# Second product of a leaky-ReLU MLP after linear attention: o of the preceding block in steps between h's, one outer Strassen product at a time over all chunks, four of seven by two levels

## The chip, the cores and the metric

One core of a Trainium2 chip. The time is the device time of one execution in microseconds (us). Its engines are named as in the profile: PE (TensorE matmul), PEld (its weight load), DVE (VectorE), ACT (ScalarE), POOL (GpSimd), SP (SyncE, which here only issues DMAs). MB are millions of bytes, KB are 1024 bytes.

## The reference, cut to what matters

```python
kv = np.einsum('bhsd,bhse->bhde', k, v)          # b=8, h=8, s=576, d=64, float32
out = np.einsum('bhsd,bhde->bhse', q, kv)
out = out / np.sqrt(np.mean(out * out, axis=-1, keepdims=True) + 1e-06) * g_norm
x = out.transpose(0, 2, 1, 3).reshape(4608, 512)
h = x @ w_in                                      # 512 x 2048
g = np.maximum(0.01 * h, h)
return g @ w_out                                  # 2048 x 512; out is 4608 x 512 float32
```

## The kernel before, in words

**Blocks and chunks.** The 4608 tokens are nine blocks of 512. For each block the kernel computes h = x w_in, g = leaky ReLU of h, and o = g w_out. The 2048 columns of h are taken in four chunks (NC) of 512: two groups of 128 from the first half of w_in's columns and two from the second. A chunk is a 2 x 2 matrix of quadrants, and so are its rows of w_out, so both products can be done by Strassen's method with seven products instead of eight. Names 11, 12, 21, 22 are quadrants; products have the numbers 1 to 7, and sums of quadrants are their operands. Block 0 is done directly, without Strassen, while the attention of the first tokens starts. Block 1 uses one level for h and for o.

**h by two levels.** From block 2 on, h of a chunk is done by two levels (`product_h_two`, line 930): seven steps, one for each inner product k, and in each step seven matmuls of 128 x 128 x 128, one for each outer product. The sums of w_in that they need are made once during block 1 (`combine`, line 702) and kept in DRAM. They come back as pieces of 448 KB, one for each step, into a ring of five places (`read`, line 737, with the DMA on line 741): when a step's matmuls are done, its place is free and SP issues the load of the piece five steps later. Results go into four PSUM banks, ha and hb or hc and hd; copies to SBUF are ACT's, adds are DVE's. Then DVE adds the outer products up to the quadrants of g, ACT applies the leaky ReLU, and POOL makes four sums of g (`sums_of`, line 839).

**o by one level, mostly.** o of a chunk (`product_o`, line 973) runs two steps of lag behind, one o step after each h step: seven products of four matmuls with 256 columns (128 x 128 weights). After every product, DVE adds the bank to the block's output quadrant in SBUF; the first chunk's are ACT's copies. The four sums of w_out's quadrants are made by POOL in block 1 and written to DRAM; from block 2 on they are read back, two DMAs of 512 KB a chunk (`sides_w2`, line 662, DMA on line 673). For 26 of the chunks, product 2 is done by two levels by the class `Second` (line 905): one more matmul of 128 columns in each h step, with its own small sums on POOL (`inner_g`, `inner_w2`) and a DVE add of 128 columns.

**Attention between.** The next block's x is made in the meantime: loads of q, k and v (lines 130 and 159; q in four DMAs for each pair of heads), DVE's transposes of q (line 455), matmuls for kv and for q kv, the norm on ACT and DVE. Steps of this work are put into fixed slots (`FINE_SLOTS`, line 1113). A slot is one h step; a block has 28. DVE and POOL then make the outer and inner sums of x (`sides_x`, line 752).

**What sets the order.** `pin` (line 90) keeps an engine's instructions in program order, so in the steady part each engine runs the order that the main loop (lines 1136 to 1222) writes down. SP issues nearly all DMAs, in one order: pieces for h, sums of w_out, loads for the attention. An issue that waits holds up those behind it.

```python
def read(to):
    nonlocal n_read
    while n_read < min(to, len(reads)):
        c, k = reads[n_read]
        pin(nc.sync.dma_start(w_place(n_read), w1_dram[c][:, SLOT[k], :, :]))
        n_read += 1
```

Of the kernel before, what the change touches and what calls it, by code (L numbers as in the profile page):

```python
# [23 lines left out]
def kernel(  # L24
# [39 lines left out]
    P = 128  # L64
# [19 lines left out]
    xpool = ctx.enter_context(tc.tile_pool(name="xpool", bufs=3))  # L84
    gpool = ctx.enter_context(tc.tile_pool(name="gpool", bufs=2))
    opool = ctx.enter_context(tc.tile_pool(name="opool", bufs=2))
# [4 lines left out]
    steady = first_done = in_line = False  # L91
# [6 lines left out]

    NW = U * NE * P
    w1_all = consts.tile([P, 2 * NC * NW], F32, name="w1_all")  # L100
    stage = consts.tile([P, 3 * NW], F32, name="stage")
    pairs = consts.tile([P, 4 * NW], F32, name="pairs")
    g_all = [consts.tile([P, 4 * U * N2], F32, name=f"g_{i}") for i in range(2)]

    def view(t, lo, *shape):
        n = 1
        for d in shape:
            n *= d
        t = t[:, lo:lo + n]
        names = "abcd"[:len(shape)]  # L110
        return t.rearrange(f"p ({' '.join(names)}) -> p {' '.join(names)}",
                           **dict(zip(names, shape))) if len(shape) > 1 else t
# [49 lines left out]
    def load_first():  # L162

        early = xpool.tile([P, NE * NT], F32, tag="xT", name="early")
# [25 lines left out]
    def make_ident():  # L190
# [9 lines left out]
    w2_sb = [[consts.tile([P, U, DM], F32, name=f"w2_{h}_{c}") for c in range(NC)]  # L200
             for h in range(2)]

    spare_homes = itertools.cycle(("gs1", "gs2", "gs3", "gs4"))

    def spare(n, name, dtype=F32):

        return gpool.tile([P, n], dtype, tag=next(spare_homes), name=name)
# [97 lines left out]
    def block(i):  # L305
        if i not in xTs:
            xTs[i] = xpool.tile([P, NE, NT], F32, tag="xT", name="xT")
        return xTs[i]
# [48 lines left out]
    def outputs(b, lo, hi, e, sums, kv=None):  # L357
# [8 lines left out]
        for l in range(2):  # L366
            sq = t2k(n, "sq" if e else f"sum{l}")
            nc.scalar.activation(sq, o_ps[l], func=AF.Square)
            if e == 0:
                sums.append(sq)  # L370
            else:
                in_turn(nc.vector.tensor_add(sums[l], sums[l], sq))
        for l in range(2):
            nc.scalar.activation(x[:, 2 * l + e, :], o_ps[l], func=AF.Copy, scale=g_sb[:, e:e + 1])

    def divide(lo, hi, sums):
# [3 lines left out]
        for l in range(2):  # L380
# [4 lines left out]
            if l:  # L385
                act = nc.scalar.activation(rms, rms, func=AF.Sqrt, scale=1.0 / D, bias=eps_sb)
                if first_done:
                    pin(act)
# [3 lines left out]
        for l in range(2):  # L392
            t = t2k(n, "spread")
            nc.scalar.copy(t.rearrange("p (a i) -> p a i", i=E),
                           rms[:, l, :].unsqueeze(2).to_broadcast([P, n // E, E]))
# [9 lines left out]
    def both_outputs(b, lo, hi, sums, kv=None):  # L405
# [8 lines left out]
        for l in range(2):  # L414
            sq = t2k(2 * n, "sq").rearrange("p (e n) -> p e n", e=2)
            nc.scalar.activation(sq, o_ps[l], func=AF.Square)
            sums.append(t2k(n, f"sum{l}"))
            in_turn(nc.vector.tensor_add(sums[l], sq[:, 0, :], sq[:, 1, :]))
        for l in range(2):
            for e in range(2):  # L420
                nc.scalar.activation(x[:, 2 * l + e, :], o_ps[l][:, e, :], func=AF.Copy,
                                     scale=g_sb[:, e:e + 1])
# [24 lines left out]
    def attention(b, apart=True, fine=False):  # L447
# [48 lines left out]
        for tail in (0, 0, 0, 0, 0, 1, 0, 0, 1, 1, 1, 1, 1, 1):  # L496
            next(tails[tail])
            yield
# [141 lines left out]
    def sides_w1(c):  # L640
# [9 lines left out]
        def more():  # L650
# [6 lines left out]
    w2_dram = [[dram.tile([P, 2, U, N2], F32, name=f"w2_{c}_{i}") for i in range(2)]  # L657
               for c in range(NC)]
    t12, t34 = pair(2, 2, U, N2), pair(3, 2, U, N2)
    writes = []  # L660

    def sides_w2(n):


# [5 lines left out]
        def sums(i):  # L670
            t = (t12, t34)[i]
            if n >= NC:
                pin(nc.sync.dma_start(t, w2_dram[c][i]))
                return
# [6 lines left out]
            if (n, i) == (NC - 1, 1):  # L681

                writes.append((w2_dram[c][i], t))
            else:
                pin(nc.sync.dma_start(w2_dram[c][i], t))
        return {1: b11, 2: b21, 3: b22, 5: t12[:, 0], 6: t12[:, 1], 7: t34[:, 0],
                4: t34[:, 1]}, sums


# [3 lines left out]
    INTO = {1: (0, 0), 2: (0, 0), 6: (0, 1), 3: (0, 1), 7: (1, 1), 5: (1, 1), 4: (1, 0)}  # L693
# [36 lines left out]
    reads = [(c, k) for _ in range(2, NB) for c in range(NC) for k in ORDER]  # L730
    RING = 5
    n_read = 0

    def w_place(n):
        return view(w1_all, n % RING * NG, 7, P)

    def read(to):
        nonlocal n_read
        while n_read < min(to, len(reads)):
            c, k = reads[n_read]  # L740
            pin(nc.sync.dma_start(w_place(n_read), w1_dram[c][:, SLOT[k], :, :]))
            n_read += 1

    qa = view(w1_all, RING * NG, 4, 4, P)
    qc = pair(0, 4, 3, P)
    xt1 = [work.tile([P, 2, N2], F32, tag="xt1", name="xt1"),
           view(w1_all, RING * NG + 24 * P, 2, N2)]
    xt24 = [work.tile([P, 2, 2, N2], F32, tag="xt24", name="xt24"),
            view(w1_all, RING * NG + 16 * P, 2, 2, N2)]
    xi = view(stage, 0, 3, 7, P)  # L750

    def sides_x(i):


        x = xTs.pop(i)
        b11, b12 = x[:, :2, :N2], x[:, :2, N2:]
        b21, b22 = x[:, 2:, :N2], x[:, 2:, N2:]
        home = i % 2 if i > 1 else 0
        t1, t2, t4 = xt1[home], xt24[home][:, 0], xt24[home][:, 1]
        if i == 1:  # L760
            t4 = opool.tile([P, 2, N2], F32, tag="o", name="xt4", bufs=6)
# [11 lines left out]
        for js, y in (((1, 7), upper), ((2, 3), lower),  # L773
                      ((6, 4), xt24[home].rearrange("p t r (v n) -> p t r v n", v=2)),
# [9 lines left out]
        def inner(kind):  # L784
            for y11, y12, y21, y22, t1, t2, t4 in batches:
                if kind == 0:
                    add(nc.gpsimd, t1, y12, y11, True)
                    add(nc.gpsimd, t2, y22, t1, True)
                elif kind == 1:
                    add(nc.gpsimd, y12, y22, y12, True)  # L790
                else:
                    add(nc.gpsimd, t4, y21, t2, True)
# [3 lines left out]
    def strassen(tags, left, right, done, order=ORDER, pieces=None):  # L796

        banks = {}  # L800
        for i in order:

            if i is None:
                yield
                continue
# [4 lines left out]
            if pieces and b == tags[0]:  # L810
                if i == 1:
                    homes = [bank] + [ps_m.tile([P, 2, N2], F32, tag=t, name=f"o_{t}")
                                      for t in ("ha", "hc")]
                    ends = [t.rearrange("p u n -> p (u n)")[:, :cols.stop - cols.start]
                            for t, (_, cols) in zip(homes, pieces)]
                for to, (part, cols) in zip(ends, pieces):
                    for r in range(2):
                        matmul(to, lhsT=left(i, part, r), rhs=right(i, part, r)[:, cols],
                               start=(i == 1 and r == 0), stop=(r == 1), skip_group_check=True)
                done(i, ends)  # L820
                yield
                continue
# [8 lines left out]
    def relu(t, src=None):  # L831
        nc.scalar.activation(t, t if src is None else src, func=AF.Prelu, alpha=SLOPE)  # L832
# [6 lines left out]
    def sums_of(c, to):  # L839

        g11, g21, g22, g12 = g_of(c)
        s1, s2, s3, s4 = (gpool.tile([P, 4, P], F32, tag=f"gs{i}", name=f"gs{i}")
                          for i in range(1, 5))
# [37 lines left out]
    gi = view(pairs, 12 * P, 4, P)  # L881

    def inner_w2(c):
        y = w2_sb[1][c]
        t1, t2, t3, t4 = (w2_sb[0][c][:, u, N2 + s * P:N2 + s * P + P]
                          for u in range(2) for s in range(2))
        y11, y12, y21, y22 = (y[:, u, s * P:s * P + P] for u in range(2) for s in range(2))
        add(nc.gpsimd, t1, y12, y11, True)
        add(nc.gpsimd, t2, y22, t1, True)
        add(nc.gpsimd, t3, y22, y12, True)  # L890
        add(nc.gpsimd, t4, y21, t2, True)

    def inner_g(c, half):

        g = g_of(c)[3]
        a11, a21, a12, a22 = (g[:, n, :] for n in range(4))
        s1, s2, s3, s4 = (gi[:, n, :] for n in range(4))
        if half == 0:
            add(nc.gpsimd, s1, a21, a22)
            add(nc.gpsimd, s2, s1, a11, True)  # L900
        else:
            add(nc.gpsimd, s3, a11, a21, True)
            add(nc.gpsimd, s4, a12, s2, True)

    class Second:


        def __init__(self, n, o, finish):
            self.n, self.o, self.finish = n, o, finish
            c = n % NC  # L910
            g, y = g_of(c)[3], w2_sb[1][c]
            ts = [w2_sb[0][c][:, u, N2 + s * P:N2 + s * P + P]
                  for u in range(2) for s in range(2)]
            self.left = {1: g[:, 0, :], 2: g[:, 2, :], 4: g[:, 3, :],
                         **{k: gi[:, at, :] for at, k in enumerate((5, 6, 7, 3))}}
            self.right = {1: y[:, 0, :P], 2: y[:, 1, :P], 3: y[:, 1, P:N2],
                          **{k: ts[at] for at, k in enumerate((5, 6, 7, 4))}}

        def product(self, k, bank):
            matmul(bank, lhsT=self.left[k], rhs=self.right[k], start=False, stop=True,  # L920
                   skip_group_check=True)

        def done(self, k, bank):
# [331 lines left out]
```

## Time and profile before

| | us |
|---|---|
| median of three runs | 917.37 (916.73 to 917.72) |
| span of the profiled execution, first to last instruction | 915.5 |
| PE busy | 909.1 |
| DVE, ACT, POOL busy | 628.2, 327.6, 367.0 |
| DMA moved in the span | 200.06 MB, mean 219 GB/s |

The profiled execution's own time is its span of 915.5 us and what lies around it, launch and end, which no instruction shows; the median of the runs is 1.9 us above the span. A row of a group of instructions reads: line, engine, operation, out<-in by the program's names, shapes, how many; then busy time and the mean of one in ns; then the engine's idle time before them and who ended it. A row of the timeline reads: start, length, engine, line, operation, operands, how many are merged. In rows of waits the first engine waited for the second: total us, times, longest. In rows of DMA issues the last number is the median time in us from issue to landing. The program's matmul in 32-bit floats appears as two MATMUL records.

### The profile page before, as it was taken

To read this page: it belongs to the slowest core of one execution; us is meant where nothing else is said; L and a number is where in the kernel's file an instruction comes from. 1 tells how busy PE (TensorE), PEld (TensorE's weight loads), DVE (VectorE), ACT (ScalarE), POOL (GpSimd) and SP (SyncE) were. 2 spreads that over 40 slices of the span, in tenths; PEclk is the share of its full clock that TensorE was granted. 3 is DMA by queue.
4 is the path that set the end of the run, shared out by engine and by line. 5 is a ranking of instruction groups with operands and counts; after the bars stand their busy time and mean duration, and the time that the engine had idled before them with its cause. 6 is when DMAs were issued, how large, how long until landed. Compare 5 with 4: busy or idle time off the path is not lost.

```text
span 915.5 us, 18030 instructions
## 1 busy us (share of the span) xinstructions
PE 909.1 (99%) x6976; PEld 775.6 (85%) x6976; DVE 628.2 (69%) x1168; ACT 327.6 (36%) x645; POOL 367.0 (40%) x440
## 2 busy tenths in 40 slices
PE   8999999999999999999999999999999999999998
PEld 5444448888998999899999999999999999999997
DVE  5876985587457876587756786678659755755565
ACT  5454533242135233533343324332343333223330
POOL 2000246977633472226321642264226422642222
DMA  9999908895599678877896689658765676667632
GB/s 267 243 243 237 239 35 258 263 304 167 175 360 286 224 213 263 235 233 211 255 261 216 219 250 263 230 179 227 224 184 176 188 221 200 184 187 223 199 107 92
DMA packets 90229, 200.06 MB, mean 219 GB/s; under 512 B 9888, under 2 KB 42272, under 8 KB 90144
## 3 DMA queue, kind: packets, MB, share of 16 engines
q1 hardware_dynamic: 79680, 187.04, 69.5%
q10 hardware_dynamic: 10016, 10.69, 3.4%
q8 instruction: 56, 0.92, 0.4%
q0 software_dynamic: 448, 1.18, 0.3%
q14 instruction: 29, 0.24, 0.1%
HBM read 172.39 MB, written 26.48 MB: 217 GB/s over the span
## 4 chain that ended last, share of the span: by engine, by line
PE 95%; DMA 2%; DVE 1%; POOL 1%; issue 0%; ACT 0%; ACTq 0%; DVEq 0%; POOLq 0%
PE o_a L118 18%; PE o_c L118 18%; PE h_ha L118 11%; PE h_hb L118 11%; PE h_hc L118 8%; PE h_hd L118 8%; PE o_acc L118 6%; PE h_ps L118 6%; PE o_ps L118 3%; PE h_a L118 1%; PE h_c L118 1%; PE kv_ps L118 1%; DMA pairs<-in_v_dram 1%; PE h_b L118 1%; PE h_d L118 1%; DMA w<-pairs 1%
## 5 line engine op out<-in xcount | busy, mean ns | idle before, releaser
L636 POOL TENSOR_TENSOR gs<-g 128x512 f32<-128x512 f32 x64 | 81.7, 1277 | 253.3 <-ACT g L832 253.3
L832 ACT ACTIVATE g<-g 128x512 f32<-128x512 f32 x124 | 78.2, 631 | 130.4 <-DVE g L636 130.4
L951 ACT COPY w_all<-h_ha 128x512 f32<-128x512 f32 x84 | 48.9, 582 | 173.9 <-PE h_ha L118 160.5
L118 PE MATMUL o_a<-pairs,gs 128*128 128x256 f32 x384 | 91.3, 381 | 0.0
L118 PE MATMUL o_c<-pairs,gs 128*128 128x256 f32 x376 | 89.2, 380 | 0.0
L636 DVE TENSOR_TENSOR o<-h_hb,o 128x128 f32<-128x128 f32 x104 | 29.8, 286 | 83.3 <-ACT pairs L951 83.2
L118 PEld LDWEIGHTS o_a<-pairs,gs 128*128 128x128 f32 x384 | 69.8, 190 | 9.2 <-POOL pairs L636 1.2
L636 DVE TENSOR_TENSOR o<-o_c,o 128x512 f32<-128x512 f32 (+1 forms) x91 | 61.1, 672 | 24.1 <-PE o_c L118 23.7
L118 PEld LDWEIGHTS o_c<-pairs,gs 128*128 128x128 f32 x376 | 68.3, 190 | 7.6
L636 DVE TENSOR_TENSOR o<-o_a,o 128x512 f32<-128x512 f32 x75 | 51.2, 682 | 28.2 <-PE o_a L118 28.1
L118 PE MATMUL h_ha<-stage,w_all 128*128 128x128 f32 x448 | 59.6, 276 | 0.0
L118 PEld LDWEIGHTS h_ha<-stage,w_all 128*128 128x128 f32 x448 | 56.6, 192 | 3.0 <-issue 0.7
L118 PE MATMUL h_ps<-xT,w_all 128*128 128x512 f32 (+1 forms) x136 | 58.1, 571 | 0.3 <-DVE w_all L258 0.3
L118 PE MATMUL o_acc<-w,g 128*128 128x512 f32 x128 | 57.7, 594 | 0.0
L636 DVE TENSOR_TENSOR g<-g,pairs 128x512 f32<-128x512 f32 x84 | 55.6, 689 | 1.9
L636 POOL TENSOR_TENSOR pairs<-g 128x128 f32<-128x128 f32 x52 | 23.7, 456 | 77.3 <-PE h_hb L118 48.5
L118 PEld LDWEIGHTS h_ps<-xT,w_all 128*128 128x128 f32 x136 | 25.4, 190 | 29.0 <-issue 26.1
L118 PEld LDWEIGHTS o_acc<-w,g 128*128 128x128 f32 x128 | 24.1, 190 | 30.2 <-issue 29.9
L636 DVE TENSOR_TENSOR w_all<-h_hc,w_all 128x512 f32<-128x512 f32 x56 | 38.3, 684 | 15.9 <-PE h_hc L118 15.6
L636 DVE TENSOR_TENSOR o<-h_hd,o 128x128 f32<-128x128 f32 x78 | 22.0, 283 | 38.2 <-ACT pairs L951 38.1
L118 PE MATMUL h_hb<-stage,w_all 128*128 128x128 f32 x336 | 46.7, 275 | 0.0
L636 POOL TENSOR_TENSOR pairs<-w 128x512 f32<-128x512 f32 x4 | 5.3, 1328 | 98.7 <-ACT cut L245 98.7
(229 smaller groups left out, 2262.4 us busy)
## 6 DMA issues: line engine op xcount, KB each, us to landing
w_all<-w SPq DMA_DIRECT2D x196, 448.0 KB, 4.2
pairs<-w SPq DMA_DIRECT2D x56, 512.0 KB, 4.3
out_dram<-o ACTq DMA_DIRECT2D x35, 256.0 KB, 4.4
v_in<-in_v_dram SPq DMA_DIRECT2D x29, 288.0 KB, 5.5
k_in<-in_k_dram SPq DMA_DIRECT2D x28, 288.0 KB, 5.3
q_in<-in_q_dram SPq DMA_DIRECT2D x56, 144.0 KB, 6.0
q_in<-in_q_dram SPq DMA_DIRECT2D x56, 140.0 KB, 6.0
w<-stage SPq DMA_DIRECT2D x12, 512.0 KB, 4.8
```

Source lines behind the costliest of these rows:

```text
L118: pin(nc.tensor.matmul(*args, **kw))
L636: ins = eng.tensor_tensor(out_, a, b_, op=ALU.subtract if minus else ALU.add)
L832: nc.scalar.activation(t, t if src is None else src, func=AF.Prelu, alpha=SLOPE)
L951: nc.scalar.copy(q[:, at], bank)
```

## The change

What it does, in the order of the new main loop:

- h as before by two levels, without the eighth matmul of `Second`. Its adds to g are done in halves: fourteen DVE adds of 256 columns a chunk (`g_sums`) instead of seven of 512.
- o of a block no longer follows chunk by chunk. The whole g of a block is kept (five quadrant tiles for each chunk), and o of block b-1 is done in 27 of block b's 28 slots, after the h step (the 28th in b-1's own last slot). Each step is one part of one outer product over all four chunks (`o_steps`, `O_STEPS`): products 2, 4 and 3 by one level, one chunk a step, four matmuls of 256 columns; products 5, 1, 6 and 7 by two levels, 28 matmuls of 128 columns in four steps of seven. They add up in PSUM over the chunks.
- The outer sums of g move from POOL to DVE (`outer_g`), and the inner sums of each two-level product are POOL's (`inner_g`, 512 columns in one or two instructions), or DVE's in the last block. Nine sums of a block's products follow at its end (`o_sums`), POOL's, in the last block DVE's.
- The two-level sums of w_out are built in blocks 2 and 3 (`w2_blocks`): product by product the outer sums are read back from DRAM, POOL makes the inner ones, and 18 writes of 256 KB by SP in block 2 and seven in block 3 put them into DRAM. From then on they are read in each block, 18 pieces of 256 to 448 KB, with product 4's outer sum among them.
- h's pieces and o's pieces share one ring of five places (`stream`, `pump`, `let_go`), in the order in which they are used.
- In block 2, o of block 1 (chunk by chunk, as before) ends in slot 6; then the slots have h alone, but for six steps of block 2's own o that are moved into it (`own[2]`). In the last block's o, 27 steps run with no h beside them.
- x's first inner sums go from POOL to DVE. Three of attention's slots in block 1 are dropped, and these steps done in block 2. Output is stored from ACT in eight parts a block, in the last block from ACT and SP.

```diff
+    def pump():
+        nonlocal n_read
+        while free_homes and n_read < len(stream):
+            piece = stream[n_read]
+            piece.home = free_homes.popleft()
+            pin(nc.sync.dma_start(view(piece.home, 0, piece.n * P), piece.src))
+            n_read += 1
...
+    KA, KB = (1, 5, 2, 4), (7, 6, 3)
+    UNITS = [(k, c) for c in range(NC) for k in KA] + [(k, c) for k in KB for c in range(NC)]
+    O_STEPS = [(2, 0), (2, 1), (4, 0), (4, 1), (2, 2), (4, 2), (4, 3), (2, 3)] \
+        + [(j, i) for j in (5, 1, 6, 7, 3) for i in range(4)]
...
+        def one_level(j, c):
+            bank = bank_of("oc" if j == 2 else "oa", c == 0)
...
+                    matmul(bank.rearrange("p (v t) m -> p v t m", v=2)[:, :, t, :],
+                           lhsT=g[:, ((Q11, Q12), (Q21, Q22))[u][t], :], rhs=w,
+                           start=c == 0 and t == 0 and u == 0, stop=True, skip_group_check=True)
...
+        def two_level(j, step):
...
+            for n in range(7 * step, 7 * step + 7):
+                k, c = UNITS[n]
...
+                matmul(bank[:, COLUMN[k], :], lhsT=left, rhs=right, start=first, stop=True,
+                       skip_group_check=True)
...
+            let_go(*end[j, i])
+            after = {5: 1, 1: 6, 6: 7}.get(j)
+            if j == 1 and i == 2:
+                for c in (2, 3):
+                    outer_g(b, 6, c, nc.vector)
+            if after and i == 2:
+                inner_g(b, after, 5, eng)
+                inner_g(b, after, 7, eng)
...
+    own = {b: {SLOTS - 1: 0} for b in range(2, NB)}
+    own[2] = {12: 0, 19: 1, 20: 2, 22: 3, 26: 4, 27: 5}
...
+    for b in range(2, NB):
+        h_now = h_steps(quarters, h_pieces[b])
...
+        for s in range(SLOTS):
+            go(h_now, 1)
...
+            if o_before(b, s) is not None:
+                o_step(b - 1)
+            if s in own[b]:
+                o_step(b)
...
+            if t == 4:
+                g_sums(b, c, 0)
+            if t == 6:
+                g_sums(b, c, 1)
...
+            if b == 2 and s >= 5 or b == 3 and s < 8:
+                go(w_steps, 1)
...
+            load_some()
...
+    b = NB - 1
+    for s in range(SLOTS - 1):
+        o_step(b)
```

## The prediction

> **What bounds the kernel now.** I read the page's busy line, its slices and the chain first: they say which engine a saving must come from.
>
> ```profile
> span 915.5 us, 18030 instructions
> ...
> PE 909.1 (99%) x6976; PEld 775.6 (85%) x6976; DVE 628.2 (69%) x1168; ACT 327.6 (36%) x645; POOL 367.0 (40%) x440
> ...
> PE   8999999999999999999999999999999999999998
> ...
> PE 95%; DMA 2%; DVE 1%; POOL 1%; issue 0%; ACT 0%; ACTq 0%; DVEq 0%; POOLq 0%
> ```
>
> PE has work in every slice and is 95% of the chain that ended last. Work taken from PE shortens the run, as long as nothing else becomes late. Ends of matmuls are modelled, so I take prices from their starts in the timeline. A matmul of the program is two records of PE there.
>
> ```profile
> 405.36 1.05 PE L118 MATMUL h_ha<-stage,w_all 128*128 128x128 f32 x8
> 406.25 0.83 PE L118 MATMUL h_hb<-stage,w_all 128*128 128x128 f32 x6
> ...
> 412.76 1.89 PE L118 MATMUL o_c<-pairs,gs 128*128 128x256 f32 x8
> 414.49 0.38 PE L118 MATMUL h_ha<-xT,w_all 128*128 128x128 f32 x2
> ```
>
> Four matmuls of 128 columns take 406.25 - 405.36 = 0.89 us, 0.2225 each; four of 256 columns take 1.73, 0.4325 each. Nothing waits between them. So an outer product of one chunk costs 4 x 0.4325 = 1.73 us by one level and 7 x 0.2225 = 1.56 by two. Next come the stages' DMA rows, since the change has many more bytes to read. Columns: length; busy time of PE, PEld, DVE, ACT, POOL; clock, DMA share, GB/s.
>
> ```profile
> 240.00:290.00 50.00, 50.00 (x490) 45.79 (x489) 29.91 (x51) 18.36 (x38) 17.41 (x20) 1.00 1.03 327
> 260.00:280.00 20.00, 20.00 (x211) 18.14 (x211) 9.86 (x16) 8.51 (x17) 5.85 (x10) 1.00 1.04 355
> 270.00:275.00 5.00, 5.00 (x50) 4.26 (x49) 1.35 (x3) 2.87 (x7) 0.00 (x0) 1.00 1.04 410
> ...
> 400.00:500.00 100.00, 100.00 (x872) 92.88 (x871) 72.36 (x140) 36.21 (x75) 38.06 (x48) 1.00 0.78 234
> ```
>
> In the steady part DMA is at 0.78. Early in block 2 it is full: 327 GB/s over 50 us, 355 over 20, 410 at best over 5. PE loses nothing there; the rows of DMA issues say why. The first is of the whole run, the others of 260 to 280 us.
>
> ```profile
> w_all<-w SPq DMA_DIRECT2D x196, 448.0 KB, 4.2
> ```
>
> ```profile
> w_all<-w SPq DMA_DIRECT2D x8, 448.0 KB, 6.8
> ...
> q_in<-in_q_dram SPq DMA_DIRECT2D x3, 144.0 KB, 8.5
> ```
>
> A piece of w_in's sums lands in 4.2 us, and in 6.8 when DMA is full. Before, five such pieces are held and one is used up in a step of h and o: 1.56 + 0.22 + 1.73 = 3.5 us. A freed place is needed again after four steps, 14 us. That cover hides even 6.8.
>
> **The change, part by part.**
>
> *PE.* The instruction listing of both kernels gives the counts. The o matmuls of 256 columns go from 784 to 448: -336 x 0.4325 = -145.3 us. Those of 128 columns go from 198 (182 beside h, 16 in the last chunk) to 784: +586 x 0.2225 = +130.4. Sum **-14.9 us**. All of it lies on the path now. It would leave 900.6 of the span of 915.5; the median of the runs, 917.37, is 1.9 above the span, so 902.5.
>
> [...] The timeline's 0.111 and 0.216 us per record are nearly in proportion to the columns, and the measurement decides.
>
> *w_out's sums.* They were made or read once a chunk: 4 reads of 512 KB a block. Now 116 blocks of 64 KB, 7.6 MB, are read per block instead of 4.2, in 18 pieces that share the five places with h's 28. During o's products 5, 6 and 7 two pieces of 448 KB are used up in 2 x 1.56 = 3.12 us: 294 GB/s, and a freed place is needed again after four pieces, **6.2 us** instead of 14. That is more than 4.2 + 0.3 (SP's issue), and less than 6.8 + 0.3.
>
> *Block 2, where o has nothing to do yet.* After block 1's o has ended (slot 5), block 2 has 23 slots of h alone (23 x 1.56 = 35.8), six o steps moved forward (6 x 1.73 = 10.4) and its attention (two kv of 1.2, products 3): 51.6 us of PE. Into the same stretch SP gets: 23 pieces of h (10.5 MB), q, k and v of the next attention (16 + 12 loads, 5.9 MB), the sums of w_out being built (18 writes of 256 KB, two reads of 1 MB: 6.8 MB), three pieces of o (1.0) and an output (0.3): 24.5 MB. At 355 GB/s that is 69 us, at 410 it is 60, at 327 it is 75. SP's order puts pieces of h behind the rest, so PE waits for the difference: 8 to 23 us, less up to 4 for what may still be in flight at the end (1.5 MB). I take 355, the best rate that held over 20 us, and the 4: 69 - 4 - 51.6 = **+13** (bounds 4 and 23).
>
> [...] No stretch of 20 us here came above 355.
>
> DVE in that stretch: adds of 512 follow each other every 0.60 us.
>
> ```profile
> 422.85 0.68 DVE L636 TENSOR_TENSOR g<-w_all 128x512 f32<-128x512 f32 x1
> 423.45 0.68 DVE L636 TENSOR_TENSOR g<-w_all,pairs 128x512 f32<-128x512 f32 x1
> 424.05 0.68 DVE L636 TENSOR_TENSOR o<-o_a,o 128x512 f32<-128x512 f32 x1
> ```
>
> A chunk has six evictions (3.3) and fourteen adds of 256, of which I have no row in this place: between 0.29 (128 columns) and 0.42 (the 256-column row of o_c), 0.34 taken, 4.8. Some 3.3 chunks make 27, attention 16, sums of g and x 9: 52 us, as much as PE. It lies beside the wait for DMA and is not added, but SP's loads of q wait for DVE's transposes (line 455), so pieces behind them are late too; that is why I take nothing off for overlap. Block 3's first five slots have h alone again, 9 us with 4.6 MB: 13 at 355, **+3** (bounds 0 and 5).
>
> *Blocks 3 to 6, q's loads among two-level steps.* In slots 7 to 10, and 15 to 18, eight pieces (3.7 MB) and two q loads (1.16 MB) fall into 12.5 us: 386 GB/s. At 355 it takes 13.6: +1.1 each; by the ring, 6.8 + 0.3 - 6.2 = 0.9 for each of the two turns it makes: +1.8. SP spends 0.42 us on each of a q load's four DMAs and waits in line:
>
> ```profile
> SPq L741 <- PE h_hb L118: 221.9, 101, 4.6
> ```
>
> SP lets a piece wait for PE, so what stands before it in SP's order delays it too. I take 1 us for each of eight groups, **+8** (bounds 0 and 18). Blocks 7 and 8 load nothing: 0, at 294 GB/s.
>
> *The rest.* ACT gets h's copies as before and loses o's; 36% busy, nothing. POOL exchanges sums of g (1.3 us each) for inner sums of the same price, some 39 us a block of 94: nothing, as long as an inner sum that waits for DVE (product 6) has the 4.9 us of the three steps beside it. If DVE is 2 us behind, PE waits. In the last block o runs alone: between products 1 and 6 two outer sums and two inner ones, 4 x 0.6 + 0.2 semaphores, stand against 1.56 + 0.22 of PE: +0.8. The nine sums at the end lie beside four steps of 1.73; the last add and store take 3 us before and after. Together **+1** (0 to 4).
>
> **Sum.** 915.5 - 14.9 + 13 + 3 + 8 + 1 = 925.6 span; with 1.9 around it **927.5 us**, 1.1% slower.
>
> **Rivals.**
>
> *DMA keeps up* (28%), the other side: the added bytes are hidden. The place is block 2, slots 5 to 27; the price of its failure is 13. It decides from 24.5 MB / (51.6 + 10) us = 400 GB/s upward, with the ring never late afterwards. For it: 410 over 5 us, and landings of 4.2 at 234 GB/s. Against it: 355 over 20 us. Time: 902.5 + 1 + 0 to 5 for block 2: 903.5 to 909, say **906**.
>
> *Only block 2 pays* (11%): blocks 3 to 6 keep their ring, since 4.2 + 0.3 is under 6.2 and a load of q is spread by the five places. Then -14.9 + 13 + 3 + 1: **919.5**; with block 2 at the mild end, 915.
>
> *The ring is late in every block* (10%): landings of 6.8 to 8.5 also in slots 19 to 22, and SP held by DVE and by eight DMA semaphores used in turn. +0.9 for each of some five turns in two-level steps a block, six blocks, is 27 instead of 8: **946**. For it: q's 8.5 us. Against it: those slots ask 294 GB/s.
>
> *It does not do what it says*: the listing shows 784 matmuls of 128 columns, so this is left out.
>
> **Numbers.** The forecast has 51% and 918 to 940 for itself; chances are 51, 28, 11 and 10. Faster by over 0.2% has the first rival and a little of the second, 0.31; within 0.2%, which is about what a measurement of this kernel can tell from no change, 0.07; slower 0.62. Cases of both signs count, so the range goes from 904 to 944.
>
> **What would show it.** Right: in the stretch of block 2 DMA share about 1 at 330 to 370 GB/s, PE idle of 10 us or more there ended by the pieces' DMA, PE busy near 894, and in blocks 3 to 6 short gaps of PE before h or o ended by DMA in slots 7 to 18. Wrong: PE without gaps in block 2 while DMA moves 400 GB/s, or gaps ended by DVE instead of DMA, or gaps at the start of product 6 ended by POOL.

## The result, and the profile after

The changed kernel takes **1013.16 us** (median of 4 runs, 1007.33 to 1014.62) against 917.55 for the kernel before (4 runs): 1.1035 times as long, with a 95% interval of 1.1005 to 1.1065. The prediction was 927.5. The direction was right, the size was not: 10.4% slower, not 1.1%, and outside the range from 904 to 944. The same views of the profile after, first the busy line, PE's slices and the chain that ended last:

```profile
span 1010.8 us, 19271 instructions
...
PE 928.0 (92%) x7476; PEld 795.6 (79%) x7476; DVE 739.7 (73%) x1261; ACT 325.3 (32%) x673; POOL 387.5 (38%) x346
...
PE   8999999999758888989988988998998999999997
...
PE 50%; DVE 24%; DMA 18%; ACT 3%; issue 2%; SPq 1%; POOL 1%; ACTq 0%; DVEq 0%; POOLq 0%
```

PE's share of the chain has gone from 95% to 50%. DMA, on which the prediction spent its working, has 18%; **DVE has 24%**, and the prediction gave it nothing. DVE is also 112 us busier than before, although it has only 93 instructions more (1261 against 1168). The groups of DVE by shape say where that lies:

```profile
L650 DVE TENSOR_TENSOR arena<-arena 128x256 f32<-128x256 f32 x460 | 242.1, 562 | 19.6 <-ACT arena L1145 12.2
L650 DVE TENSOR_TENSOR arena<-arena 128x512 f32<-128x512 f32 x161 | 161.0, 1026 | 12.6 <-PE o_a L129 7.6 <-PE o_c L129 1.0 <-ACT arena L804 0.9
...
L650 DVE TENSOR_TENSOR arena<-h_hc,arena 128x512 f32<-128x512 f32 x42 | 28.8, 686 | 63.1 <-PE h_hc L129 60.0 <-ACT arena L1145 3.1
```

An add of 512 columns with one input in PSUM (h_hc) takes 0.69 us, as before. The same add with both inputs in SBUF (arena<-arena) takes 1.03; before it was 0.69 as well (the rows of g). The 256-column ones average 0.56, where the prediction took 0.34. The timeline of the end of block 5, DVE and POOL, shows why; x8 is eight instructions in a row:

```profile
643.51 9.04 DVE L650 TENSOR_TENSOR arena<-arena 128x512 f32<-128x512 f32 x6
...
643.67 13.36 POOL L650 TENSOR_TENSOR arena<-arena 128x512 f32<-128x512 f32 x8 [1.10 <-DVE arena L650]
...
653.54 5.09 DVE L650 TENSOR_TENSOR arena<-arena 128x512 f32<-128x512 f32 x5
...
659.73 2.81 DVE L650 TENSOR_TENSOR arena<-arena 128x256 f32<-128x256 f32 x7
```

While POOL makes the column sums of o at 13.36 / 8 = 1.67 us each, DVE's six adds take 1.51 each, more than twice 0.69: they go in turns. When POOL is done, DVE's adds of 256 columns follow each other every 0.40 us. PE pays at once, in the same stretch:

```profile
653.21 1.16 PE L129 MATMUL h_ha<-arena 128*128 128x128 f32 x8 [2.07 <-DVE arena L650]
...
659.28 1.98 PE L129 MATMUL h_hc<-arena 128*128 128x128 f32 x8 [2.52 <-DVE arena L650]
```

The next table sorts DVE's adds over the whole trace by whether a POOL instruction ran during them (median, us; worked out from the starts and ends in the trace). "Beside" means that POOL ran for at least 95% of the add; adds that met POOL for a smaller part are in no column.

```
                     both inputs in SBUF            one input in PSUM
                     alone          beside POOL     beside POOL
before, 512 cols     0.68 (x211)    1.14 (x9)       0.68 (x102)
after,  512 cols     0.69 (x76)     1.64 (x51)      0.69 (x44)
after,  256 cols     0.42 (x353)    0.94 (x40)
```

Before, the two engines hardly met (23 of 234 adds of 512 columns with both inputs in SBUF, 91 of 167 after): POOL's sums of g needed what DVE's adds had just made, so they came after them. The change put sums on both engines that don't need each other.

The stages, with the columns of the prediction (length; busy PE, PEld, DVE, ACT, POOL; clock, DMA share, GB/s):

```profile
240.00:290.00 50.00, 39.36 (x406) 35.99 (x406) 31.48 (x63) 10.99 (x26) 5.71 (x6) 0.91 0.77 248
...
250.00:338.00 88.00, 67.02 (x640) 60.57 (x638) 57.79 (x113) 23.96 (x52) 13.37 (x10) 0.86 0.88 284
...
280.00:300.00 20.00, 10.32 (x139) 8.11 (x138) 1.75 (x3) 6.28 (x14) 5.00 (x4) 0.76 1.00 341
450.00:550.00 100.00, 91.79 (x879) 86.09 (x864) 77.68 (x126) 33.18 (x74) 42.39 (x36) 0.98 0.83 257
```

In block 2 PE has half its time idle in the worst 20 us, with DMA at 1.00 and 341 GB/s, near the 355 of the prediction, and the granted clock down to 0.76. DVE is nearly idle there: this place is DMA's. Over the whole stretch from 250 to 338 us, though, DMA is at 0.88 and 284 GB/s, so a full DMA alone doesn't make block 2's loss. In the steady part both are short.

From here on a slot's **loss** is its length, from its first h matmul to the next slot's, less its own matmuls at the prediction's prices. By blocks, with the three runs that matter most beside the changed kernel:

```
block                      2     3     4     5     6    7    8    sum
changed kernel           33.2  22.8  12.8  16.2  11.4  7.0  1.0  104.4
  slots 15, 25 to 27      2.8   7.6   7.1   8.2   7.0  6.6  1.1
  slots 10, 11, 17, 18    0.6   9.6   5.5   7.5   4.6   0    0
e1, no GpSimd adds       32.7  14.7   5.4  12.2   4.0  0.2 -0.2   69.0
e2, q not loaded         32.9  13.4   8.2  10.1  10.8  6.9  1.0   83.3
e7, nothing beside       10.5   1.9   0.0   0.0   0.0  0.2 -0.2   12.4
```

(In block 5 slot 9 loses another 0.5 to q.) With the prediction's 900.6 for PE's saving alone, 104.4 and 3.8 at the end make 1008.8 of the span of 1010.8; the other 2 us lie ahead of block 2 or in rounding.

### The profile page after: what moved, and what is told of

It is laid out like the page before. It is cut to its first block, busy times and chain, and to the rows that moved or that the text cites. A ratio compares the mean times of both kernels' runs of the same rounds, so it can differ in the third digit from the quotient of the medians.

```text
span 1010.8 us, 19271 instructions
## 1 busy us (share of the span) xinstructions
PE 928.0 (92%) x7476; PEld 795.6 (79%) x7476; DVE 739.7 (73%) x1261; ACT 325.3 (32%) x673; POOL 387.5 (38%) x346
## 4 chain that ended last, share of the span: by engine, by line
PE 50%; DVE 24%; DMA 18%; ACT 3%; issue 2%; SPq 1%; POOL 1%; ACTq 0%; DVEq 0%; POOLq 0%
DVE arena L650 22%; PE o_a L129 14%; PE o_c L129 9%; DMA arena<-w 5%; PE h_hc L129 5%; PE h_ha L129 5%; DMA q_in<-in_q_dram 4%; PE h_hb L129 3%; PE h_hd L129 3%; DMA arena<-in_moe_w_in_dram 3%; DMA v_in<-in_v_dram 3%; DMA arena<-in_moe_w_out_dram 2%; PE o_acc L129 2%; PE o_ps L129 2%; PE h_ps L129 2%
## 5 line engine op out<-in xcount | busy, mean ns | idle before, releaser
L650 POOL TENSOR_TENSOR arena<-arena 128x512 f32<-128x512 f32 (+2 forms) x330 | 380.6, 1172 | 565.1 <-DVE arena L650 196.9
L650 DVE TENSOR_TENSOR arena<-arena 128x256 f32<-128x256 f32 (+2 forms) x649 | 410.3, 668 | 32.5 <-ACT arena L1145 12.2
L129 PE MATMUL o_a<-arena 128*128 128x128 f32 (+1 forms) x1456 | 249.0, 318 | 8.4 <-DMA arena<-w 8.0
L129 PEld LDWEIGHTS o_a<-arena 128*128 128x128 f32 x1456 | 211.7, 193 | 22.3 <-issue 5.8
L129 PE MATMUL o_c<-arena 128*128 128x128 f32 (+1 forms) x1008 | 164.9, 312 | 9.5 <-DMA arena<-w 9.5
L129 PEld LDWEIGHTS o_c<-arena 128*128 128x128 f32 x1008 | 142.6, 193 | 18.3 <-DMA arena<-w 10.8
L129 PE MATMUL h_hc<-arena 128*128 128x128 f32 x784 | 109.7, 285 | 20.2 <-DVE arena L650 11.2
L129 PE MATMUL h_ha<-arena 128*128 128x128 f32 x784 | 109.0, 283 | 17.4 <-DVE arena L650 11.2
L129 PEld LDWEIGHTS h_hc<-arena 128*128 128x128 f32 x784 | 100.8, 198 | 28.4 <-DVE arena L650 14.4
L129 PEld LDWEIGHTS h_ha<-arena 128*128 128x128 f32 x784 | 99.6, 196 | 26.3 <-DVE arena L650 18.1
L1145 ACT COPY arena<-h_hc 128x512 f32<-128x512 f32 x56 | 33.2, 592 | 202.6 <-PE h_hc L129 105.4
```

The lines of the kernel that those rows point to most:

```text
L129: pin(nc.tensor.matmul(*args, **kw))
L650: ins = eng.tensor_tensor(out_, a, b_, op=ALU.subtract if minus else ALU.add)
L1145: act(nc.scalar.copy(q[:, to], bank))
```

## The experiments

Theory **D** is the prediction's: DMA, in block 2 and behind q. Theory **V**: DVE's adds with two SBUF inputs and POOL's adds hold each other up. The changed kernel's own times lie 7 us apart, and each experiment is one run (the kernel before, run beside them, took 916.6 to 918.6), so a difference of 5 us means something only where the slots' losses show it too.

**e1: GpSimd's adds left out from block 3's slot 8 on.**

```diff
     def add(eng, out_, a, b_, minus=False, pinned=False):
+        if light and eng is nc.gpsimd:
+            return
```

> From slot 8 of block 3 on every add of GpSimd is left out (inner sums of g and x, the column sums of o at a block's end), so the output is not the reference's; VectorE, PE and all DMAs stay. Theory V (VectorE's adds with both inputs in SBUF and GpSimd's adds hold each other up): VectorE's 512-column SBUF adds fall from 1.03 to 0.69 us and the 256-column ones from 0.56 to 0.42, the losses of PE in slots 15 and 25 to 27 of blocks 3 to 8 (7.6, 7.1, 8.2, 7.0, 6.6, 1.1 us) go, and the time falls by about 38 to 975 us. Theory D (the DMA of block 2 and of q's loads, as predicted): nothing of that changes, 1008 to 1013 us.

974.26 us, 38.9 less, as V has it (2.4 of it lie ahead of block 2, where nothing was changed; the slots named next make 37.6). DVE's busy time falls from 740 to 641 us. The losses in slots 15 and 25 to 27 are gone in every block from 3 to 8; those of slots 10, 11, 17 and 18 stay. From 345 us to the last h step, first the changed kernel, then e1:

```profile
L650 DVE TENSOR_TENSOR arena<-arena 128x512 f32<-128x512 f32 x114 | 122.4, 1100 | 2.7 <-PE o_a L129 0.4
```

```profile
L652 DVE TENSOR_TENSOR arena<-arena 128x512 f32<-128x512 f32 x114 | 75.8, 691 | 3.0 <-PE o_a L129 0.9
```

The same 114 instructions cost 47 us less when nobody is beside them.

**e4: the same adds replaced by two fills each.**

```diff
+        if light and eng is nc.gpsimd:
+            for _ in range(2):
+                pin(eng.memset(out_, 0.0))
+            return
```

> As the kernel without GpSimd's adds from slot 8 of block 3 on, but each left-out add is replaced by two fills of its output with zeros, so GpSimd is busy, writes SBUF and still makes its readers wait, but reads nothing from SBUF (the output is not the reference's). Theory V in the form that only GpSimd's reads hold VectorE up: VectorE's adds stay at 0.69 and 0.42 us, the time is that of the kernel without the adds, about 975 us. If GpSimd's writing or the waits for GpSimd cost the time: 1000 us or more, and VectorE's adds stay at 1.03 and 0.56.

978.63 us. In the same stretch GpSimd's 404 fills make 170 us of work, and DVE's rows stay clean:

```profile
L654 DVE TENSOR_TENSOR arena<-arena 128x512 f32<-128x512 f32 x114 | 76.0, 693 | 2.9 <-PE o_a L129 0.9
...
L652 POOL MEMSET arena<- 128x512 f32 x244 | 125.0, 524 | 320.9 <-PE o_a L129 179.5 <-PE o_c L129 67.8 <-DVE arena L654 56.7
```

So it is not that GpSimd works, writes, or is waited for. What a fill leaves out of an add is the sum itself and that it *reads* SBUF; and of DVE's adds only those that read two SBUF inputs get slower (1.64 us beside POOL's adds against 0.69, with one input in PSUM 0.69 beside them too). The price is 1.64 - 0.69 = 0.95 us, most of a POOL add (1.27 alone), and at the end of block 5, from 644 to 653 us, the two engines' adds end in turn, one of POOL's and one of DVE's. What in the hardware makes them take turns, no run shows.

**e15: a dose of it in the kernel before.** One more POOL add of 448 columns per slot from block 2 on, on a tile nobody else uses.

```diff
+                if not one:
+                    add(nc.gpsimd, extra, extra, extra, True)
```

> The kernel before with one more GpSimd add of 448 columns, both inputs in SBUF, on a tile that nobody else uses, in each of the 28 slots of blocks 2 to 8; all its work is done. GpSimd gets some 196 x 1.15 = 225 us, to 65% busy; PE, DMAs and VectorE's instructions stay. Theory V: VectorE's 512-column SBUF adds, 0.686 us at 249 of 282 places before, become 1.0 to 1.7 us at a third or more of them, VectorE's busy time rises from 628 by 50 to 100 us, its adds with an input in PSUM stay at 0.68, and the time rises to 922 to 950 us. Theory D: VectorE's rows stay as they were; 917 to 920 us.

928.09 us against 916.58, 1.3% more, without a change in what PE, DVE or DMA are given to do. Before, then with the dose:

```profile
L636 DVE TENSOR_TENSOR g<-g,w_all 128x512 f32<-128x512 f32 x56 | 38.4, 686 | 2.9
```

```profile
L638 DVE TENSOR_TENSOR g<-g,w_all 128x512 f32<-128x512 f32 x56 | 44.6, 797 | 2.9
...
L638 DVE TENSOR_TENSOR w_all<-h_hc,w_all 128x512 f32<-128x512 f32 x56 | 38.3, 684 | 16.0 <-PE h_hc L120 16.0
```

89 of the 234 adds of 512 columns with both inputs in SBUF now meet a POOL add, 23 before, at some 1.0 us each (the expectation's 282 include wider adds); adds from PSUM don't notice. DVE's busy time rose by 29 us, less than the 50 expected. The kernel before pays the price too, so it doesn't come from the changed kernel's order.

**e2: q not loaded from attention 4's third pair on.**

```diff
+        if (b, p) > (4, 1):
+            q_ins[b, p] = q_kept[p % 2]
+            return
```

> q is no longer loaded from the third pair of attention 4 on (block 3's slots on); the transposes read the last two tiles, so the output is not the reference's. 14 loads of 4 DMAs, 8 MB, are gone. Theory D: the losses in slots 10, 11, 17 and 18 of blocks 3 to 6 (9.6, 5.5, 8.0, 4.6 us) go, the time is about 985 us. Theory V: only what the transposes waited for is gained, 1005 to 1013 us, and slots 25 to 27 keep their 5 to 7 us of loss in each block.

988.77 us, 24.4 less, close to D's 985. The losses in slots 10, 11, 17 and 18 go; slots 15 and 25 to 27 keep theirs. D and V are thus both true, each in its own slots.

**e9 and e12: the same bytes of q in another form**, two DMAs of 288 KB or four of 144 KB, but to all 128 partitions.

```diff
-                pin(nc.sync.dma_start(t[r0:r0 + 32, :n], src[:, 32 * c:]))
+            pin(nc.sync.dma_start(t[:, l * J * D:(l + 1) * J * D],
+                                  q[b, 2 * p:2 * p + 2].rearrange("h (p j) d -> (h p) (j d)", j=J)))
```

> The same bytes of q are loaded at the same places, but in two DMAs of 288 KB to 128 partitions, the form in which k and v are loaded, in place of four of 144 KB to 32 partitions each (the tile's contents are then not q as the attention wants it, so the output is not the reference's). If it is q's bytes that make the pieces behind them late: slots 10, 11, 17 and 18 of blocks 3 to 6 keep their loss, 1008 to 1013 us. If it is the form, since k and v with as many bytes cost nothing: nearly as without q, 989 to 995 us, and the pieces' landing falls from 7 to 8.7 us behind q to about 5.

> The bytes of q at the same places in four DMAs of 144 KB, as in the changed kernel, but each to 128 partitions (contents not q as the attention wants it, so the output is not the reference's). Two DMAs of 288 KB to 128 partitions gave 994.2 us, four to 32 partitions 1013. If the number of DMAs is the cause: 1006 to 1013 us. If the 32 partitions are: 990 to 997 us.

994.20 and 997.42 us. Most of what q costs is the form, 32 partitions to a DMA, and not its bytes or the number of DMAs; some 2 us a block in slots 10, 11, 17 and 18 stay. Issues from 345 us to the end of block 6, the changed kernel and then e9:

```profile
q_in<-in_q_dram SPq DMA_DIRECT2D x28, 144.0 KB, 7.3
...
k_in<-in_k_dram SPq DMA_DIRECT2D x12, 288.0 KB, 4.8
```

```profile
q_in<-in_q_dram SPq DMA_DIRECT2D x28, 288.0 KB, 5.8
```

The trace's DMA packets have the price: a packet of 4480 or 4608 bytes of q occupies a DMA engine for 0.30 us (15 bytes/ns), one of 3584 bytes of a piece for 0.14 (25.6 bytes/ns), medians from 345 to 770 us. All 16 engines are busy, at 226 GB/s, against 376 when only pieces are under way:

```profile
480.00:483.00 3.00, 3.00 (x29) 3.00 (x29) 1.34 (x3) 3.00 (x8) 1.43 (x2) 1.00 1.00 226
...
489.00:493.00 4.00, 2.93 (x26) 2.77 (x26) 3.73 (x9) 0.00 (x0) 0.01 (x1) 1.00 1.01 376
```

Pieces issued behind eight such DMAs landed after 7 to 9 us, while the ring covers 6.2. The length of q's packets is not the cause: 15% of those of 4480 bytes take 0.17 us (25.9 bytes/ns) in the same stretch, and in e16 below, where few engines work, 57 GB/s at a DMA share of 0.15 are 24 bytes/ns to a busy engine. q's rate is six tenths of the pieces', per packet (15 against 25.6) and in all (226 against 376). Why 32 partitions have this price, no run shows.

**e10 and e13: q by ScalarE's queue**, at the same place, or three slots later.

```diff
-                pin(nc.sync.dma_start(t[r0:r0 + 32, :n], src[:, 32 * c:]))
+                pin((nc.scalar if b > 2 else nc.sync).dma_start(t[r0:r0 + 32, :n], src[:, 32 * c:]))
```

> From attention 3 on q's four DMAs are issued by ScalarE's queue, not by SyncE's; bytes, form and slots stay, and all work is done. If the pieces are late because they stand behind q in SyncE's line: 988 to 995 us. If they are late because q's packets take the DMA engines' time, whatever queue they come from: 1006 to 1013 us. ScalarE spends 1.7 us more a load on issuing, and waits where a tile of q is still being read; if that decides, 1015 us or more.

> q's four DMAs from attention 3 on by ScalarE's queue as before, but each load three slots later, so that the tile it overwrites has long been read and ScalarE doesn't wait for VectorE; all work is done. With ScalarE's queue at the old place PE hardly waited for pieces in blocks 3 to 8, but 24 us for ScalarE. If that wait was all that took the gain: 985 to 996 us. If q's DMAs hold up pieces from any queue once they overlap more of them: 1005 us or more.

1027.13 and 1014.89 us. In e10 PE waited for ScalarE instead, 24 us from block 3 on, since ScalarE's copies stood behind DMAs that waited for a tile to be read. Three slots later that is 4 us, and PE still waits 11 us for pieces (20 in the changed kernel). The expectation of 985 to 996 was wrong: blocks 3 to 6 lose 5 us less than in the changed kernel, and block 2 loses 10 more, since PE waits 12.5 us for ScalarE there. So SP's line makes the pieces late for a part at most. That q's packets take the DMA engines' time from any queue agrees with the rest, but these two runs, with ScalarE's waits in them, don't show it alone.

**e3, e5 and e6: block 2.** e3 leaves out the writes and reads by which w_out's sums are built; e5 leaves out POOL's adds from block 2's slot 5 on; e6 both.

```diff
     def w2_write(j, k, src):
...
-        pin(nc.sync.dma_start(to, src))
```

> The w_out sums that block 2 makes are neither written nor is their source read back (18 DMAs of 256 KB, later ones too, and three reads of 1 MB are gone); GpSimd still adds; o's pieces are read from another DRAM tensor in the same sizes, so the output is not the reference's. Theory D: block 2 has 6.8 MB less at 355 GB/s, 19 us of its 33 us of loss go, and some of block 3's 23: 985 to 994 us. Theory V: block 2's loss is VectorE's, at most 5 us go: 1008 us.

> GpSimd's adds are left out from slot 5 of block 2 on, not only from block 3 (those of the w_out sums in blocks 2 and 3 are replaced by one fill each; the output is not the reference's). All DMAs stay. If VectorE and GpSimd holding each other up is also what block 2 loses by: its losses in slots 22 to 27 (8 us) and block 3's in slots 1 to 6 (5 us) go against the kernel without the adds from block 3 on (974.3), 961 to 965 us. If block 2 loses by DMA alone: 972 to 976 us.

> No GpSimd adds from slot 5 of block 2 on, and the w_out sums neither written nor their source read (o's pieces are read from another DRAM tensor; the output is not the reference's). Without the writes alone PE lost 7 us in slot 6 to VectorE beside eight GpSimd adds that no longer waited for a DMA; here that can't be. If the 6.8 MB cost block 2 what the prediction said (13 to 19 us of its 33): block 2 loses 14 to 20 us, 945 to 950 us. If block 2 loses by the loads of k and v, which PE waits for, or by SP's order: 957 us or more.

1011.33, 973.94 and 963.34 us. e3 misled when taken alone: block 2 loses 29.0, not 33.2, because POOL's eight adds no longer wait for a DMA and run into DVE's in slot 6, where PE loses 7.1. With POOL out of the way (e5, block 2 33.0) the same edit takes block 2 to 20.0 (e6): 13 us for w_out's DMAs (10.6 in the whole run). Of what V was expected to cost there, 8 us in slots 22 to 27 of block 2 and 5 in slots 1 to 6 of block 3, only 1 and 2 us went, and e5 is no faster than e1. So 20 us of block 2 have another cause.

**e7: e6, and no load of k, v and q from attention 3's third pair on.**

> As the kernel without GpSimd's adds and without the w_out sums' DMAs, and also without any load of k, v and q from the third pair of attention 3 on (the attention computes with the tiles loaded before; the output is not the reference's). What is left on SP is the pieces of h and o. If the three causes (VectorE with GpSimd, loads of attention, DMAs of the w_out sums) are all there is, every block has PE's own time: span 900.6 by the prediction's PE term and up to 4 at the end, 903 to 908 us. If the pieces alone are late in two-level steps: 915 us or more, with gaps of PE ended by the pieces' DMA in blocks 4 to 8.

917.73 us: 45.6 less than e6, and just the time of the kernel before. Blocks 4 to 8 have no loss, so PE's prices and the pieces of o were right. The expectation was 903 to 908; it was missed by 10.5 us of block 2 and 1.9 of block 3. There DMA is at 0.60 and PE waits for ACT and DVE (3.3 and 3.8 us are named in the waits, the rest is not): a slot with h alone is 1.56 us of PE, and its two evictions and g's sums don't always fit beside it.

**e8 and e11: the work placed otherwise, all of it done.** e8 gives g's inner sums to DVE; e11 makes g's sums in seven adds of 512 columns.

```diff
     def o_eng(b):
-        return nc.vector if b == NB - 1 else nc.gpsimd
+        return nc.vector
```

> All work stays; the inner sums of g that GpSimd makes in blocks 3 to 7 (some 16 adds of 512 columns a block) go to VectorE; x's sums, the column sums of o and w_out's sums stay on GpSimd. Theory V: fewer adds collide, so VectorE's busy time hardly grows although it has 80 adds more, the losses in slot 15 (1.1 to 1.6 us a block) go, those of slots 25 to 27 stay: 1000 to 1006 us. Theory D: VectorE has 11 us a block more and nothing is gained: 1010 to 1025 us.

> g's sums are made in seven adds of 512 columns in the chunk's last slot, as in the kernel before, not in two times seven of 256; all work is done. Alone 7 x 0.69 is 1.1 us less a chunk than 14 x 0.42. If a collision costs VectorE one GpSimd add, about 1.1 us, whatever the width of VectorE's add, fewer adds collide less often: block 2's and the ends' losses shrink, 995 to 1006 us. If only columns count: 1008 to 1013 us. If ScalarE, which must then wait with the next chunk's first copy for all seven, comes to decide: slower than 1013 us.

1007.79 and 1019.44 us. e8 has 116 DVE instructions more and DVE's busy time is 7 us higher; slot 15's loss is gone, the ends are as they were. In e11 DVE's busy time falls by 42 us and the kernel is not faster: slot 15 now loses 2.9 to 3.9 us. The timeline at that place in block 8's slots:

```profile
915.46 10.52 DVE L650 TENSOR_TENSOR arena<-arena 128x512 f32<-128x512 f32 x10 [1.21 <-PE o_a L129]
916.23 6.67 POOL L650 TENSOR_TENSOR arena<-arena 128x512 f32<-128x512 f32 x4 [7.20 <-DVE arena L650]
...
924.87 0.59 ACT L1145 COPY arena<-h_ha 128x512 f32<-128x512 f32 x1 [8.82 <-DVE arena L650]
...
925.51 2.08 PE L129 MATMUL h_ha<-arena 128*128 128x128 f32 x8 [2.71 <-ACT arena L1145]
```

DVE's ten sums meet POOL's four inner ones; ACT may not copy the next chunk's bank over their operands until they are done, 8.82 us, and PE then waits 2.71 us for the bank. Busy time saved elsewhere is worth nothing here.

**e14, e16, e17, e18: toward a repaired kernel.** e14 is e13 with e8's edit. e16 loads each head's two copies of q by one DMA to 64 partitions, e17 adds e8's edit, e18 gives all of POOL's adds to DVE.

```diff
+            src = bass.AP(tensor=src.tensor, offset=src.offset, ap=[[32, 2], *src.ap])
+            pin(nc.sync.dma_start(t[64 * l:64 * l + 64, :n], src))
```

> q by ScalarE's queue three slots later, and g's inner sums on VectorE; all work is done. The second part alone gave 5.4 us less. If the two causes are apart, their gains add: 980 to 990 us. The kernel before stays faster: what block 2 and the blocks' ends lose is still there, some 33 and 6 x 6 us.

> All work is done and q arrives as the attention wants it, but each head's two copies come in one DMA of 280 KB to 64 partitions, two DMAs a pair in place of four to 32 partitions. If few partitions to a DMA are the cause: between the forms of 128 (994 to 997 us) and of 32 (1013), 997 to 1004 us. If only the whole 128 help: 1008 us or more.

> q in two DMAs to 64 partitions each, and g's inner sums on VectorE; all work is done. The second alone gave 5.4 us less. If the two causes are apart the gains add: 990 to 999 us.

> As with g's inner sums on VectorE, and also the inner sums of x and the column sums of o at a block's end: GpSimd has nothing to do from block 3's slot 8 on; all work is done. If it is the two engines' holding each other up that costs the ends of the blocks: VectorE's SBUF adds are all at 0.69 and 0.42 us, the ends lose at most what VectorE's 20 us more work a block cost, 970 to 985 us. If VectorE, with some 94 us of work in a block of 94 us of PE, is then itself the bound: slots 23 to 27 lose 6 to 10 us a block as before, 990 to 1010 us.

1004.25, 1234.57, 1230.51 and 1221.19 us. e14 is 10.6 us faster than e13, but block 2 loses 10 us more than in the changed kernel, as in e13, and the expected 980 to 990 was missed. The 64-partition form was a bad miss; while q loads, e16 has

```profile
606.00:614.00 8.00, 1.51 (x14) 1.32 (x12) 2.47 (x4) 1.07 (x3) 1.08 (x1) 0.88 0.15 57
```

a DMA share of 0.15: the work of two to three of the 16 engines, 57 GB/s, and the pieces behind wait: PE loses 161 us to them in the whole run. The source's outermost dimension has two entries; whether that or the 64 partitions is the cause was not shown. Within this group V can still be read, away from q: in slots 15, 25 to 27 and the next slot 0 of blocks 3 to 7 e18 loses 22 us, e16 35. DVE has 218 instructions more in e18, some 20 us a block, and its busy time is only 4 us higher (741 against 737). More than a third of this loss is gone; that the rest is then DVE's own work is likely and not shown. No version that does all the work beat the kernel before.

## Why the prediction was wrong, point by point

The sum lacked one part and had most others too small; the runs put these sizes on them:

| step of the prediction | predicted | measured |
|---|---|---|
| PE | -14.9 | blocks 4 to 8 as priced (e7: loss 0.0); PE busy 898.0 in e7 against 909.1 before |
| block 2, w_out's sums and the rest | +13 (4 to 23) | 33.2: 13 w_out's DMAs (e6 against e5), 9.5 attention's loads (e7 against e6), 10.5 h alone with ACT and DVE |
| block 3's first five slots | +3 (0 to 5) | 3.5, but 2 of it stay in e7, without these DMAs |
| blocks 3 to 6, q | +8 (0 to 18) | 24 (e2) |
| the rest: DVE "beside", POOL "nothing" | +1 (0 to 4) | 38 (e1, slots 15 and 25 to 27), and 3.8 at the end |

**The step that failed** is the one on DVE and POOL: DVE's work "lies beside the wait for DMA and is not added", POOL "exchanges sums of g (1.3 us each) for inner sums of the same price, some 39 us a block of 94: nothing". Each engine was asked whether it has the time, and both had. Nobody asked whether they can work at the same time. Its row for DVE's adds, 0.60 us apart, came from a place where POOL was idle. For 256 columns the text says "I have no row in this place" and takes 0.34 between 0.29 and 0.42; alone such an add takes 0.42. There was a row, at another place of the same trace of before (block 1), in which POOL ran beside six of the eight adds:

```profile
L636 DVE TENSOR_TENSOR stage<-w_all 128x256 f32<-128x256 f32 x8 | 8.0, 1002 | 0.0
```

1.00 us for 256 columns, where 512 took 0.69 elsewhere: 0.42 for the two adds that were alone, 0.94 to 1.49 for the six. That row had the whole price in it.

**Block 2** had DMA as a cause rightly, and its size too small. The prediction's 13 was for all of the stretch's bytes; that w_out's DMAs alone measured 13 is chance, since the attention's loads, which its 24.5 MB include, cost 9.5 more. Its 355 GB/s was not the best rate that held over 20 us: from 256 to 276 us the trace of before has 377. It let PE wait for pieces only. PE itself waits for the loads of v, 10.6 us in three waits in block 2 of the changed kernel:

```profile
PE o_ps L129 <- DMA v_in<-in_v_dram: 5.6, 2, 3.2
PE kv_ps L129 <- DMA v_in<-in_v_dram: 5.0, 1, 5.0
```

And slots of h alone are too short for their evictions: 10.5 us, put at nothing.

**q** was right in place (slots 7 to 10 and 15 to 18; the losses appear two or three slots later) and in the wait, pieces that come late behind q, and mis-sized twice. 355 GB/s was used for bytes that move at some 226. "The ring, 6.8 + 0.3 - 6.2" should have had 7 to 9 us of landing. The groups are seven, not eight (14 loads, two to a group), and cost some 3.5 us each, not 1. The 8.5 us for q stood in the prediction's own fence. A slip without effect: the kernel before reads w_out's sums eight times 512 KB a block, not four; the 4.2 MB are right.

**The end** was "3 us before and after": the span ends 6.9 us after PE's last matmul, 3.1 before. The last two stores are issued behind six others.

**What was to show it wrong** did: gaps "ended by DVE instead of DMA". From 345 us on PE waits 20.6 us for DVE's sums and 20.4 for pieces. Of the signs for right, PE busy near 894 (928) and a full DMA over all of block 2's stretch (0.88, 284 GB/s) did not come. Of the rivals, "DMA keeps up" and "only block 2 pays" fell; "the ring is late in every block" (946) came nearest, but by luck: its 27 us were to come from the ring in blocks without q too, and blocks 7 and 8 have no such loss. In no rival did DVE become late, although the change gave it the outer sums of g and x's first inner sums.

## What to carry to other kernels

Before moving sums to an engine that "has time", ask what the others will be doing beside it: here DVE's adds with two SBUF inputs cost more than double when they meet POOL's adds (0.69 to 1.64 us), and POOL's a quarter more (1.27 to 1.6). An order in which one needs the other's result, as in the kernel before, kept them apart (23 of 234 such adds met POOL's, 91 of 167 after). Take an operation's price from all its rows in the trace, and look hard at one that is dear at one place and cheap at another. A load's cost to those behind it was its time on the DMA engines, not its bytes: the same bytes of q made the kernel 1013 us long in DMAs to 32 partitions, and 994 and 997 in DMAs to 128. Look up a load's packets in the trace before counting its bytes.

## What the runs showed of the hardware that was not expected

- DVE adds of 512 and 256 columns with both inputs in SBUF: 0.69 and 0.42 us alone, 1.64 and 0.94 (medians) with POOL's adds beside; with POOL's fills in their place (e4) 0.69 and 0.43 in the mean, as without (e1); of 512 columns with one input in PSUM 0.68 to 0.69, with POOL beside or not.
- A DMA of 144 KB to 32 partitions: 0.30 us of an engine for a packet of 4608 bytes, against 0.09 for 2304 (25 bytes/ns) of one to 128 partitions (k and v). To 64 partitions with an outermost dimension of 2 (e16): a DMA share of 0.15, 57 GB/s.
- The granted clock was 0.76 from 280 to 300 us, where PE was idle half the time, and 0.98 from 450 to 550. After five of PE's waits, of 2.2 to 3.6 us, the next eight matmul records of h took 1.94 to 2.08 us (2.05 at 277.62 us), after the others, of 0.2 to 2.8 us, 1.13 to 1.16, and 1.06 in a stream (128 columns each): those five waits cost about 1 us more than their own length.
